# Two raw FFN weight transfers issued ahead of the second batch's v in a fused attention and FFN kernel

## The chip, the cores and the metric

The kernel runs on one core of a Trainium2 chip. Its time is the device time of one execution in microseconds (us), and the kernel before has a median of 1057.45 us in three runs (1054.2 to 1062.04). A profiled execution gives the trace from which all rows below come.

## The reference: what is computed

Three stages follow each other. All arrays are float32, except that the two FFN weights come as float64.

1. Attention on q, k, v of shape (2 batches, 8 heads, 576 positions, 64). Each head adds two attentions: a *pooled* one, on q, k, v averaged over groups of four positions (144 by 144 scores), whose output rows are repeated four times, and a *local* one, in which a position sees only the positions less than four away.
2. An FFN on the 1152 x 512 result: `h = x @ w_in` (512 x 2048), softplus of h, times `w_out` (2048 x 512).
3. Eight experts (512 to 1024 to 512, ReLU), all applied to all tokens and summed with weights P, which come from gate logits by eight rounds of row and column normalization.

## The kernel before

**Stages.** TensorE does the attention of both batches first, then the FFN in four blocks of 512 hidden units, then the experts. The last two take most of the time; the diff touches a load in the attention.

**The attention's units.** Work is cut into units: `pooled(b, hf, p)` (half of the pooled rows, two heads) and `local(b, t, g)` (a tile of 116 positions, four heads). Each has four steps s1 to s4: scores and row maxima and exponentials (`softmax_exp`, VectorE line 306, ScalarE line 309), transposes (TensorE lines 335 and 397, copied by ScalarE at 337 and 399), products with v (lines 344 and 406), and a last transpose (lines 361 and 426). The last step of a pooled unit is copied by ScalarE into `upT` (line 362); that of a local unit is added to it by VectorE into `xf` (line 433, two buffers), which GpSimd splits into two float32r halves of `x` (lines 446 and 447). `emit` lays the units out as a pipeline: with each new unit's s1 come s2 of the unit two back, s3 of the one four back and s4 of the one six back. `fill` and `warm` add products of zeros on TensorE.

**What is hung between the units.** The dictionary `at` holds work to be put in front of the n-th unit: at 1 the q and k of batch 1 (`load_second`), at 9 `load_rest`, at 11 to 14 the pooling of q and k of batch 1 (`pool_qk`), at 16, 19, 23 and 29 the preparation of the first four tiles of FFN weights (`prep`), and from 22 on the first FFN products.

**load_rest.** `load_vd(1)` loads v of batch 1 in two halves `vr` of 80 x 2048 float32 (line 293, 640 KB each) and lets GpSimd add the four positions of each group: line 296 gives `vs`, line 298 the pooled `vd`. The two `vs` lie in the scratch buffers with the tags `ch` and `cs`:

```
s = self.convp.tile([GH, 2, DM], F32, tag=("ch", "cs")[hf], name=f"vs{b}{hf}", bufs=1)
```

`load_raw(1)` issues the loads of the raw weight tiles 0 and 1 (line 117, 1024 KB each, float64 read as pairs of 32-bit words) into two buffers that v of batch 0 has used before them. All four loads are issued by SyncE.

**prep.** `from_double` turns a raw tile into two float32r halves. ScalarE reads it twice, at line 133 into `cs` and at line 135 into `cm`; VectorE works on `cm` (136, 138), then writes `ch` from the raw tile (139), and goes on with 142 to 144; GpSimd ends with line 146 for the first four tiles. `cm`, `ch` and `cs` have one buffer each, which the `vs` of batch 1 share for the latter two. `prep` also orders its work behind a local unit: ScalarE's part behind that unit's copy (line 399), VectorE's behind its add (line 433).

**Who sets the order.** Each engine runs its instructions in a fixed order, which a planner writes when the kernel is built: it goes through the program with durations of its own for every instruction and transfer, and gives each engine, whenever it is free, the first instruction in source order whose inputs and buffers it then reckons to be ready. So an engine's order is not the source's where something comes late by the planner's reckoning. On the chip an instruction that is not ready holds up all that is behind it on its engine.

Of the kernel before, what the change touches and what calls it, by code (L numbers as in the profile page):

```python
# [80 lines left out]
class Net:  # L81
# [660 lines left out]
    def run(self):  # L742
# [52 lines left out]
                self.load_qk(1, p)  # L795

        def load_rest():
            self.load_vd(1)
            self.load_raw(1)

        def prep(n, lag):

# [225 lines left out]
```

## Time and profile before

| | |
|---|---|
| median of three runs | 1057.45 us (1054.2, 1057.45, 1062.04) |
| profiled execution, its own time | 1064.65 us |
| its span, first to last instruction | 1062.9 us |
| TensorE busy | 1050.3 us, 99% of the span |
| VectorE, ScalarE, GpSimd busy | 775.2, 428.7, 162.5 us |
| bytes read by transfers | 60.51 MB |

The page gives the span in 40 slices of 26.6 us, the chain of waits that ended last, and groups of instructions; other views list the instructions of an engine in order of time, or the busy time, the granted TensorE clock and the transfer rate of a stretch. An idle time in brackets is that of the engine just before the instruction, with what ended it. Times count from the span's start.

### The profile page before, as it was taken

Reading aid. Unit: us, or ns where it says so; the run is one execution under the profiler, and the core shown is the slowest. Engines: PE = TensorE matmul, PEld = TensorE weight load, DVE = VectorE, ACT = ScalarE, POOL = GpSimd, SP = SyncE. Lnnn points to the kernel's source line nnn. Section 1 sums busy time; section 2 is a strip of 40 time slices with the busy share of each in tenths; the row PEclk is TensorE's granted clock in tenths of the full one; section 3 lists DMA queues with packets and bytes.
Section 4 is the critical chain, followed back from the end, with each engine's and each line's share of the span. In section 5 each row is a group of like instructions: output and inputs, shape, how many; then the busy total and the mean of one; then the engine's idle time right before and its main releaser. Section 6 shows DMA issues by size and latency. Waiting matters only on the chain.

```text
span 1062.9 us, 16399 instructions
## 1 busy us (share of the span) xinstructions
PE 1050.3 (99%) x6570; PEld 945.1 (89%) x6570; DVE 775.2 (73%) x1470; ACT 428.7 (40%) x815; POOL 162.5 (15%) x210
## 2 busy tenths in 40 slices
PE   8999999999999999999999999999999999999998
PEld 5667999999998899898989989898998989899897
DVE  6578699999987687784947658494765848576572
ACT  5567697776743433241413324141331414133130
POOL 2653300002112220111202011120201112020000
PEclk9789999999999999999999999999999999999999
DMA  9532032222111221111211111121111112110003
GB/s 286 167 97 75 2 119 80 80 80 80 40 40 40 80 80 40 40 41 40 80 40 41 40 40 40 40 81 40 40 40 41 41 40 80 41 40 1 1 2 89
DMA packets 14348, 63.92 MB, mean 60 GB/s; under 512 B 1792, under 2 KB 4608, under 8 KB 7808
## 3 DMA queue, kind: packets, MB, share of 16 engines
q1 hardware_dynamic: 13696, 61.70, 17.9%
q8 instruction: 51, 0.84, 0.3%
q10 hardware_dynamic: 576, 1.18, 0.3%
q14 instruction: 25, 0.20, 0.1%
HBM read 60.51 MB, written 2.36 MB: 59 GB/s over the span
## 4 chain that ended last, share of the span: by engine, by line
PE 89%; DVE 5%; DMA 3%; ACT 2%; issue 1%; SPq 0%; DVEq 0%; ACTq 0%
PE po L613 37%; PE pu L564 33%; PE ph L471 7%; PE py L513 6%; DMA raw<-in_w 1%; DMA k<-in_k 1%; PE pvl L406 1%; PE pl L385 1%; DMA vw<-in_vw 1%; DVE h L492 1%; PE pxl L426 1%; DVE r L488 1%; DVE l L489 1%; DVE yp L525 0%; PE pd L320 0%
## 5 line engine op out<-in xcount | busy, mean ns | idle before, releaser
L564 PE MATMUL pu<-T,a 128*128 128x320 f32 (+1 forms) x2688 | 354.6, 293 | 1.4 <-DVE yp L525 1.4
L564 PEld LDWEIGHTS pu<-T,a 128*128 128x128 f32 x2688 | 351.7, 188 | 3.0 <-issue 1.7
L613 PE MATMUL po<-w,h 128*128 128x512 f32 x960 | 221.3, 390 | 0.0
L635 DVE SCALAR_TENSOR_TENSOR acc<-po,prob,acc 128x512 f32<-128x512 f32 x126 | 94.1, 748 | 173.6 <-PE po L613 173.6
L613 PEld LDWEIGHTS po<-w,h 128*128 128x128 f32 x960 | 179.9, 188 | 37.3
L197 ACT CAST w<-raw 128x1024 fp32r<-128x1024 f32 x32 | 33.4, 1052 | 271.4 <-PE po L613 271.4
L613 PE MATMUL po<-w,h0a 128*128 128x512 f32 x576 | 142.3, 390 | 0.5 <-DVE w L198 0.5
L166 POOL TENSOR_TENSOR s<-raw 128x256 f32<-128x256 f32 x32 | 28.6, 892 | 677.9 <-DVE a L177 472.8
L613 PEld LDWEIGHTS po<-w,h0a 128*128 128x128 f32 x576 | 107.3, 188 | 22.4 <-DVE w L198 0.9
L513 PE MATMUL py<-h,w 128*128 128x384 f32 x576 | 104.0, 336 | 0.6 <-DVE l L490 0.3
L471 PE MATMUL ph<-x,w 128*128 128x384 f32 x576 | 104.4, 336 | 0.0
L513 PEld LDWEIGHTS py<-h,w 128*128 128x128 f32 x576 | 99.7, 188 | 1.7 <-DVE h L492 0.8
L471 PEld LDWEIGHTS ph<-x,w 128*128 128x128 f32 x576 | 99.7, 188 | 0.6 <-issue 0.4
L576 ACT ACTIVATE h<-c 128x320 fp32r<-128x320 f32 x128 | 58.6, 468 | 80.2 <-DVE c L587 80.2
L577 DVE SCALAR_TENSOR_TENSOR h<-c,h 128x320 fp32r<-128x320 f32 x128 | 67.9, 539 | 0.3
L587 DVE TENSOR_TENSOR c<-v,pu 128x256 f32<-128x256 f32 (+1 forms) x128 | 57.6, 450 | 10.9 <-PE pu L564 7.9
L576 ACT ACTIVATE h0a<-c 128x256 fp32r<-128x256 f32 x96 | 37.5, 417 | 50.3 <-DVE c L587 50.0
L198 DVE TENSOR_TENSOR w<-raw,w 128x1024 fp32r<-128x1024 f32 x32 | 39.0, 1219 | 22.1 <-ACT w L197 22.1
L613 PE MATMUL po<-w,h0b 128*128 128x512 f32 x192 | 54.3, 389 | 0.0
L613 PEld LDWEIGHTS po<-w,h0b 128*128 128x128 f32 x192 | 36.0, 188 | 7.5
L585 ACT COPY p<-pu 128x256 f32<-128x256 f32 (+1 forms) x64 | 25.2, 393 | 36.8 <-PE pu L564 35.1
L577 DVE SCALAR_TENSOR_TENSOR h0a<-c,h0a 128x256 fp32r<-128x256 f32 x96 | 39.0, 419 | 0.8 <-ACT h0a L576 0.5
(139 smaller groups left out, 1207.8 us busy)
## 6 DMA issues: line engine op xcount, KB each, us to landing
raw<-in_w SPq DMA_DIRECT2D x48, 1024.0 KB, 4.9
vw<-in_vw SPq DMA_DIRECT2D x20, 130.0 KB, 4.1
vr<-in_vp SPq DMA_DIRECT2D x4, 640.0 KB, 10.3
k<-in_k SPq DMA_DIRECT2D x8, 288.0 KB, 6.6
out<-acc SPq DMA_DIRECT2D x5, 256.0 KB, 2.0
q<-in_q ACTq DMA_DIRECT2D x4, 288.0 KB, 5.9
q<-in_q SPq DMA_DIRECT2D x4, 288.0 KB, 7.1
out<-acc SPq DMA_DIRECT2D x8, 128.0 KB, 2.3
```

Of the source, the lines that this page charges most:

```text
L166: nc.gpsimd.tensor_tensor(s[:, 0], a21, a22, ALU.add)
L197: nc.scalar.copy(w[:, 0], raw)
L198: nc.vector.tensor_tensor(w[:, 1], raw, split(w[:, 0]), ALU.subtract)
L471: nc.tensor.matmul(ps[:, i], lhsT=wv[:, a, k, fo : fo + P], rhs=x[:, b, k], start=(n == 0), stop=(n == 3 * KD - 1),)
L513: nc.tensor.matmul(ps[:, a], lhsT=w[:, i, d * P : (d + 1) * P], rhs=h[:, j, f], start=(n == 0), stop=(n == 3 * NFT - 1),)
L564: nc.tensor.matmul(ps, lhsT=w[:, x, a, k], rhs=t[:, y, b, k], start=(m == 0), stop=(m == 5))
L576: act = nc.scalar.activation(hi, src, AF.Relu)
L577: dve = nc.vector.scalar_tensor_tensor(lo, src, 0.0, split(hi), ALU.max, ALU.subtract)
L585: nc.scalar.copy(to, ps)
L587: nc.vector.tensor_tensor(to, src, ps, ALU.add)
L613: nc.tensor.matmul(ps, lhsT=self.h[s, i, f][:, at * P : (at + 1) * P], rhs=w[:, j], start=(n == 0), stop=(n == 3 * NFT - 1),)
L635: nc.vector.scalar_tensor_tensor(acc, ps, pe, acc, ALU.mult, ALU.add)
```

## The change

Inside `load_rest` the two calls change places, so that the loads of raw weight tiles 0 and 1 stand in front of the loads and additions of the second batch's v. Nothing else is edited.

```
         def load_rest():
+            self.load_raw(1)
             self.load_vd(1)
-            self.load_raw(1)
```

## Rows read from the trace of the kernel before

**Rows 1.** The page's slices: granted TensorE clock in tenths of full speed.
```profile
PEclk9789999999999999999999999999999999999999
```

**Rows 2.** Stretches: from:to, length, busy us of each engine (instructions), granted clock, transfers' share, GB/s.
```profile
38.60:59.02 20.42, 20.42 (x143) 13.27 (x142) 12.80 (x31) 11.13 (x35) 10.86 (x10) 0.50 0.21 66
...
59.02:130.00 70.98, 70.87 (x659) 56.91 (x659) 55.89 (x151) 49.88 (x141) 31.53 (x44) 1.00 0.22 65
...
130.00:160.00 30.00, 30.00 (x175) 30.00 (x174) 29.02 (x36) 26.11 (x32) 0.00 (x0) 1.00 0.32 106
```

**Rows 3.** TensorE in order of time: start, length, line, operation, [idle before, released by].
```profile
24.51 0.27 PE L374 MATMUL pl<-mask,identb 128*128 128x256 bf16 x1
...
33.53 0.28 PE L374 MATMUL pl<-mask,identb 128*128 128x256 bf16 x1
...
35.10 0.66 PE L406 MATMUL pvl<-vw,ptls 128*64 128x130 f32 x8
38.06 0.44 PE L426 MATMUL pxl<-perm,ull 128*128 128x128 f32 x2 [2.29 <-ACT upT L362]
38.60 0.37 PE L374 MATMUL pl<-mask,identb 128*128 128x256 bf16 x1
...
58.66 0.42 PE L374 MATMUL pl<-mask,identb 128*128 128x256 bf16 x1
...
67.33 0.67 PE L344 MATMUL pvd<-vd,ptds 72*72 72x65 f32 x8
...
71.06 0.44 PE L471 MATMUL ph<-x,w 128*128 128x384 f32 x1
```

**Rows 4.** ScalarE in order of time.
```profile
30.81 0.94 ACT L309 ACTIVATE e<-pl,nm 128x64 f32<-128x64 f32 x4
32.99 0.40 ACT L337 COPY ptds<-ptd 72x288 f32<-72x288 f32 x1 [1.24 <-PE ptd L335]
36.77 1.13 ACT L135 ACTIVATE cm<-raw 128x1024 f32<-128x1024 f32 x1 [3.39 <-DMA raw<-in_w]
37.81 0.19 ACT L362 COPY upT<-pxd 128x72 f32<-128x72 f32 x1
...
41.37 1.16 ACT L133 ACTIVATE cs<-raw 128x1024 f32<-128x1024 uint32 x1
```

**Rows 5.** SyncE's queue in order of time: issues merged (x2), from the first's start.
```profile
19.94 2.47 SPq L293 DMA_DIRECT2D vr<-in_vp  x2
22.91 1.09 SPq L117 DMA_DIRECT2D raw<-in_w  x2
```

**Rows 6.** The second raw transfer alone, from issue to landing.
```profile
DMA to landing us min/median/max: 16.1/16.1/16.1
```

**Rows 7.** Stretches again, while v and then the raw tiles pass; last two columns count.
```profile
25.00:31.00 6.00, 5.88 (x73) 4.02 (x71) 2.85 (x10) 4.67 (x18) 0.81 (x2) 1.00 1.00 240
31.00:36.00 5.00, 4.77 (x56) 3.18 (x52) 3.76 (x12) 1.14 (x5) 4.23 (x2) 1.00 1.02 369
```

**Rows 8.** VectorE in order of time.
```profile
16.02 1.22 DVE L296 TENSOR_TENSOR vs<-vr 72x1024 f32<-72x1024 f32 x1 [0.71 <-DMA vr<-in_vp]
...
38.60 0.40 DVE L433 TENSOR_TENSOR xf<-pxl,upT 128x232 f32<-128x232 f32 x1 [2.41 <-ACT e L309]
...
42.56 1.23 DVE L139 SCALAR_TENSOR_TENSOR ch<-raw,cm 128x1024 int32<-128x1024 int32 x1
```

**Rows 9.** GpSimd in order of time.
```profile
31.25 2.35 POOL L296 TENSOR_TENSOR vs<-vr 72x1024 f32<-72x1024 f32 x1 [3.75 <-DMA vr<-in_vp]
34.11 2.34 POOL L296 TENSOR_TENSOR vs<-vr 72x1024 f32<-72x1024 f32 x1 [0.52 <-DMA vr<-in_vp]
36.42 1.27 POOL L298 TENSOR_TENSOR vd<-vs 72x512 f32<-72x512 f32 x1
...
38.40 0.38 POOL L446 CAST x<-xf 128x232 fp32r<-128x232 f32 x1
38.73 1.27 POOL L298 TENSOR_TENSOR vd<-vs 72x512 f32<-72x512 f32 x1
```

## The prediction

> **What bounds the kernel now.** I read the page's slices first, 26.6 us each. TensorE's granted clock is at 9 tenths or more in every slice but the second and third [rows 1], so a change to the opening can act on time in two ways: by a wait, or by the clock. The stretches [rows 2] place the loss: from 38.60 to 59.02 us the granted clock is 0.50 (1.2 of 2.4 GHz), afterwards 1.00, and TensorE is busy for all 20.42 us of it. The list of TensorE in order of time [rows 3] shows what came before the fall: nothing runs between the values of 35.10 and the transposes at 38.06, which record 2.29 us of idle time and name ScalarE as the releaser. ScalarE's list [rows 4] names the source: it is free at 33.39, and its next instruction, line 135 on the first raw weight tile, starts at 36.77 after 3.39 us of idle time ended by the transfer. The copy that TensorE needs stands right behind it and starts at 37.81. SyncE's list [rows 5] has the two transfers of v of batch 1 (line 293) from 19.94 and the two raw ones (line 117) from 22.91 on; each row merges two issues, the second of them some 0.35 us before the row's end. The first raw tile is there at 36.7, the second 16.1 us after its issue at 23.65 [rows 6], at 39.8. They are late because of what is ahead of them: the transfer engines are full from 25 to 36 us, at 240 GB/s while v's 1.31 MB pass and at 369 while the raw 2.1 MB pass [rows 7].
>
> From 130 us on TensorE has no gaps (30.00 of 30.00 us busy, at full clock) [rows 2]. Time won or lost in the opening therefore arrives at the end whole, since all later work is started by work and by no fixed hour.
>
> **The change, part by part.** No instruction is added. Six things move past each other: two raw issues on SyncE go ahead of two v issues, and the four additions of lines 296 and 298 on GpSimd stay where they are in the source, with their data later. The memset of the ones column reads nothing and is not affected.
>
> *Issue slots.* The four SyncE issues take about 0.35 us each [rows 5] in either order, and what is queued behind them on SyncE, the windows of v for the local attention, keeps its slot. A raw tile needs a buffer that v of batch 0 leaves; its second reader on VectorE starts at 16.02 and runs 1.22 us [rows 8], so 17.24 is before the slot at 19.94: no new wait.
>
> *Landing.* v lands at 31.2 and 34.1 (that is when line 296 starts, each after a wait on the transfer) [rows 9], 2.9 us apart; raw follows 2.6 and 3.1 us apart. So the queue reaches v at about 28.3. In the new order I put raw 0 at 28.3 + 2.6 to 3.1 = 30.9 to 31.4, raw 1 at 34, v at 37 and, the bytes being the same, the last at 39.8 as before. Raw 0 is 5.5 us earlier; both v tiles 5.7 us later.
>
> *ScalarE's wait.* With raw 0 there at 31, line 135 (1.13 us) is ready inside the 1.24 us that ScalarE idles between its exponentials (end 31.75) and 32.99 [rows 4]. The 3.39 us wait goes, and so do TensorE's 2.29 us. Bounds: a planner orders the engines by readiness as it foresees it; it placed line 135 where the tile came 3.4 us too late. If it now places it as much too early, the gain is nothing; if it fits, 2.29. I take 2.29, because a free slot lies right behind the new landing.
>
> *The clock.* If TensorE does not stop, I expect it not to fall. What that gives back: five units lie between the starts of the local units at 38.60 and 58.66, 20.06 us or 4.01 each; before the fall, the four from the local unit at 24.51 to that at 33.53 take 9.02, or 2.26 each [rows 3]. Five at 2.26 are 11.3 us, so 20.06 - 11.3 = 8.8 us come back. The lower bound is nothing (the clock falls anyway); a bound between comes from VectorE, which is busy for 12.80 us in the same stretch [rows 2]: if that work must fit, 20.42 - 12.80 = 7.6 us. I take 8.8, since conversion work on VectorE is not wanted by TensorE at once and may slide.
>
> The Trainium skill (TensorE: Matmul & The Clock Gate, Terms) prices throttled time at its length times one minus the granted share; for these 20.42 us at half clock that is an estimate of 10.2 us, and the sum would be 1.4 us better by it. The rows of the units, which contain waits that do not scale with the clock, say 8.8, and I keep them.
>
> *v's own path.* The sums need v at 37 and 39.8: two of 2.35 us and two of 1.27 [rows 9] end at about 43.4 and 44.7 instead of 37.7 and 40.0. The reader on TensorE of the pooled v of batch 1 comes at 67.33 [rows 3], some 56 in the forecast: covered by 11 us. Not covered are two uses of the same scratch. The sums live in the buffers that the weight conversion then writes: line 139 on VectorE (42.56 now [rows 8]) cannot start before the first pooled sum is through, line 133 on ScalarE (41.37 now [rows 4]) not before the second. These are late next. If the planner moves them behind the later v, they cost nothing; if not, see the first rival. Bounds: 0 to 3.8 us of TensorE idle; I take 0.
>
> Sum, against the profiled execution's own time: 1064.65 - 2.3 - 8.8 = 1053.6 us. That execution is 7.2 us above the median of the three runs shown (1057.45), whose lowest is 1054.2; a spread of that size in a kernel that is otherwise saturated is what a half-clock stretch of varying length would give. If the lowest run had no such stretch, only the wait is left to win there: 1054.2 - 2.3 = 1051.9. The two stand near each other, and the forecast between them is **1053 us**, 0.4% under the median.
>
> **Rivals.** *The wait moves to v* (about 1058). At the present spacing VectorE reaches line 139 4.0 us after its add at 38.60 at half clock, some 2.5 at full; without the stop this is 39 to 40. The first sum is through at 43.4, so VectorE would stand for 3 to 4.5 us, with the row maxima of the softmax behind it in order, ScalarE's exponentials behind these and TensorE last. Now 3.39 + 1.13 us of ScalarE's time cost TensorE 2.29, so some 2.2 us are covered; 0.9 to 3.8 us of TensorE idle time would come at 44. With a stop like the present one the clock falls too, and the profiled sum is 1064.65 - 2.29 + (0.9 to 3.8) = 1063.3 to 1066.2, no difference to speak of: 1056 to 1059 on the scale of the median. For it: the transfers are the same bytes in the same full queue, and somebody must be last. Against it: the planner does let readiness decide (it runs line 135 before line 133, against the source), so it can shift lines 133 and 139 too. The Trainium skill (DMA: Bandwidth & Descriptors, Issuing engines are not separate DMA queues) holds that transfers from all queues run on the same engines; by that rule reordering only names another victim, which is this rival.
>
> *GpSimd's queue is blocked* (about 1065, slower). If GpSimd keeps its order, the split of the first attention output (38.40 now) stands behind both additions of line 296 and the first of line 298 [rows 9] and moves 5.7 us to 44.1. The output that it reads has two buffers, so VectorE's third add of this kind (line 433), due at 36.3 + 2 x 2.26 = 40.8, waits until some 46: 5 us, of which 2.2 are covered, so 2.8 of TensorE idle time for the present 2.29. If the clock then stays low up to the first FFN matmuls, the 12 us from 59.02 to 71.06 [rows 3] grow by 12 x (4.01 / 2.26 - 1) = 9.3, and the 5.5 us between 38.6 and 44 at full clock give back 2.4: 1057.45 + 0.5 + 9.3 - 2.4 = 1064.9. It decides if the splits stay behind the v sums; that the first split has its data before v lands in the new order, and so may pass it by readiness, speaks against it.
>
> *The order does not change what ScalarE waits for* (about 1057): the planner places line 135 as much ahead of the new landing as of the old one.
>
> **How the numbers follow.** Forecast 0.45, wait moves to v 0.30, GpSimd blocked 0.14, nothing changes 0.11. The range takes in the forecast with both bounds of the clock term and the two neutral rivals: 1051.9 less 3 for runs on the good side, 1049, up to 1064 for the milder half of the blocked queue. One per cent, about what a measurement of this kernel can tell from no change, is 10.6 us: faster than 1046.9 needs the whole forecast against runs of before as long as the slowest shown, about a third of its 0.45, so 0.16; slower than 1068 is the blocked queue with more idle time than reckoned, most of its 0.14, 0.11; within, 0.73.
>
> **What would show it.** Right: line 135 starts by 33 with no wait for a transfer, TensorE has no gap over 1 us between 30 and 46, the clock is at 1.00 in 40 to 59, the first FFN matmul comes at about 60 instead of 71. Wrong: a gap on TensorE at 40 to 46 behind line 139 or 133 (first rival), the third output add of VectorE waiting on GpSimd (second), line 135 still waiting for its transfer (third), or a clock that falls with no gap ahead of it.

## The result: slower by 0.7%, not faster

The changed kernel takes 1067.9 us (median of 9 executions, 1065.3 to 1069.1); the kernel before 1061.4 (9, 1054.2 to 1063.4). The ratio is 1.0068, interval 1.0044 to 1.0092. The forecast of 1053 us and its range up to 1064 were wrong, and so was the sign.

What the change was to do, it does. SyncE's queue after (start, length, issues merged):

```profile
20.44 1.59 SPq L117 DMA_DIRECT2D raw<-in_w  x2
22.40 1.07 SPq L293 DMA_DIRECT2D vr<-in_vp  x2
```

ScalarE after, against [rows 4]: line 135 runs at 28.70 with no wait ahead of it, and line 133 without one as well.

```profile
28.70 1.14 ACT L135 ACTIVATE cm<-raw 128x1024 f32<-128x1024 f32 x1
...
44.10 1.23 ACT L133 ACTIVATE cs<-raw 128x1024 f32<-128x1024 uint32 x1
```

TensorE after, every instruction of 30 to 110 us with more than 0.5 us of idle time ahead of it (in brackets, with the releaser), against [rows 3]. Line 220 is a product of zeros that `fill` puts in; `uld` (line 356) and `ull` (line 420) are the outputs of a pooled and of a local unit, which VectorE writes and TensorE transposes:

```profile
38.75 0.38 PE L220 MATMUL ptl<-z 128*128 128x512 bf16 x1 [0.51 <-DVE ull L420]
41.98 0.39 PE L220 MATMUL ptl<-z 128*128 128x512 bf16 x1 [0.73 <-DVE uld L356]
48.55 0.59 PE L220 MATMUL pvl<-z 128*128 128x512 bf16 x1 [1.54 <-DVE uld L356]
62.37 2.58 PE L471 MATMUL ph<-x,w 128*128 128x384 f32 x12 [0.69 <-POOL x L446]
77.70 0.44 PE L335 MATMUL ptd<-ident,e 72*72 72x72 f32 x4 [1.55 <-DVE uld L356]
97.71 0.25 PE L361 MATMUL pxd<-ident,uld 72*128 72x72 f32 x1 [1.82 <-DVE uld L356]
```

The one gap of 2.29 us behind ScalarE is gone; six others stand in its place, and five of them wait for VectorE. In the opening TensorE is well ahead: the first FFN matmul comes at 62.37 instead of 71.06. The stretches after (columns as in [rows 2]) show where that went:

```profile
48.75:55.34 6.59, 6.59 (x44) 4.02 (x44) 5.99 (x12) 3.79 (x10) 4.16 (x3) 0.50 0.51 187
55.34:79.22 23.88, 21.64 (x210) 16.08 (x210) 20.38 (x50) 17.15 (x46) 16.16 (x18) 1.00 0.34 111
79.22:85.97 6.75, 6.75 (x39) 5.67 (x40) 3.78 (x13) 3.07 (x9) 0.64 (x1) 0.50 0.17 43
...
99.85:106.73 6.88, 6.88 (x44) 6.08 (x43) 2.30 (x8) 2.44 (x10) 1.28 (x4) 0.51 0.16 41
```

The clock falls to half three times, each time within 2.2 us of the end of one of the three longest gaps, for 6.59 + 6.75 + 6.88 = 20.2 us together, as much as the single 20.42 us of [rows 2]. So in these two executions nothing of the clock is won, and TensorE has more holes. Over the stretch from 30 to 130 us it is idle for 6.84 us instead of 2.50, at a mean granted clock of 0.90 in both; the kernel before, then after:

```profile
30.00:130.00 100.00, 97.50 (x864) 74.24 (x864) 73.06 (x195) 64.51 (x186) 49.22 (x59) 0.90 0.26 83
```

```profile
30.00:130.00 100.00, 93.16 (x840) 72.10 (x841) 77.37 (x189) 60.67 (x178) 49.18 (x57) 0.90 0.25 72
```

Why VectorE is late, its own list and GpSimd's show. VectorE after:

```profile
35.84 2.52 DVE L136 TENSOR_SCALAR cm<-cm 128x1024 f32<-128x1024 f32 x1
38.28 0.41 DVE L420 TENSOR_TENSOR ull<-pvl,rrl 128x256 f32<-128x256 f32 x1
...
38.95 2.18 DVE L138 TENSOR_SCALAR cm<-cm 128x1024 int32<-128x1024 int32 x1
...
45.22 1.74 DVE L142 TENSOR_SCALAR ca<-raw 128x1024 int32<-128x1024 int32 x1
...
74.80 0.41 DVE L306 TENSOR_REDUCE nm<-pl 128x4 f32<-128x256 f32 x1
...
75.42 2.02 DVE L488 SCALAR_TENSOR_TENSOR r<-r,e 128x384 f32<-128x384 f32 x1
77.37 0.28 DVE L356 TENSOR_TENSOR uld<-pvd,rrd 72x128 f32<-72x128 f32 x1
...
94.75 2.61 DVE L488 SCALAR_TENSOR_TENSOR r<-r,e 128x384 f32<-128x384 f32 x1
```

GpSimd after:

```profile
35.46 5.12 POOL L296 TENSOR_TENSOR vs<-vr 72x1024 f32<-72x1024 f32 x2 [2.05 <-DMA vr<-in_vp]
...
74.66 2.37 POOL L146 TENSOR_TENSOR w<-cs,ch 128x1024 fp32r<-128x1024 f32 x1 [5.23 <-DVE ch L144]
...
94.60 2.35 POOL L146 TENSOR_TENSOR w<-cs,ch 128x1024 fp32r<-128x1024 f32 x1 [5.43 <-DVE ch L144]
```

These long instructions of VectorE start while one of GpSimd's is running (35.84 after 35.46; 75.42 after 74.66; 94.75 after 94.60), and the two of line 488 end 0.4 us behind its end (75.42 + 2.02 = 77.44 against 74.66 + 2.37 = 77.03; 97.36 against 96.95). In the kernel before, line 136 takes 0.68 us in three of the first four tiles, and line 488 takes 0.53 to 0.55 us up to 110 us. VectorE before, the first two of line 136:

```profile
38.92 1.63 DVE L136 TENSOR_SCALAR cm<-cm 128x1024 f32<-128x1024 f32 x1
...
55.36 0.68 DVE L136 TENSOR_SCALAR cm<-cm 128x1024 f32<-128x1024 f32 x1
```

Not every instruction of VectorE is held: line 306, which reads PSUM, takes its usual 0.41 us at 74.80, inside the same GpSimd instruction that holds line 488. The attention's small operations stand behind the held ones in VectorE's order. At 78 and 98 us uld comes next and TensorE waits for it; at 48 us VectorE has had no pause since 35.5, has spent 2.52, 2.18 and 1.74 us on lines 136, 138 and 142, which take 0.68 alone, and reaches uld late. That is the theory that the experiments test. The rival: the planner, given earlier raw tiles, puts VectorE's conversion work ahead of the attention's, and this order alone makes TensorE wait.

**Two terms.** The kernels' times spread by up to 10 us from execution to execution, so each execution is split in two below: its *clock loss*, (1 - mean granted clock) x span, and the *rest*, its time less that. This is bookkeeping and not a cause, but it separates the two things that the change touches. The kernel before, 87 executions beside the runs below: clock loss 4.7 us on average (0 to 12.8), rest 1054.4. In 23 of the 87 the clock is at 0.999 or more, with the same program; their mean is 1055.3 us. The split takes off a little too much: over the 87, a straight line through times and losses rises by 0.81 us for each us of clock loss, so a rest measured at much loss comes out too low. The changed kernel: 8.9 and 1058.7. So of its 8.5 us over the mean of the 87 (1067.6 against 1059.1), about half are clock and half stalls (at 0.81 us each, 3.4 and 5.1).

| kernel | ratio to before [interval] | clock loss, us | rest, us |
|---|---|---|---|
| changed kernel | 1.0068 [1.0044, 1.0092] | 8.9 | 1058.7 |
| 1 new transfers, old order | 1.0055 [1.0029, 1.0081] | 9.5 | 1055.5 |
| 2 old transfers, new order | 1.0147 [1.0115, 1.0179] | 13.6 | 1061.6 |
| 3 before, line 135 later | 1.0028 [0.9998, 1.0058] | 7.4 | 1054.8 |
| 4 changed, all cut in four | 1.0038 [1.0019, 1.0057] | 6.8 | 1056.7 |
| 5 changed, line 146 cut | 1.0021 [1.0000, 1.0042] | 3.0 | 1057.6 |
| 6 changed, sums in place | 1.0117 [1.0082, 1.0152] | 12.8 | 1057.7 |
| 7 the same, planned anew | 1.0000 [0.9979, 1.0022] | 3.4 | 1055.2 |
| 8 as 3, sums in place | 0.9971 [0.9951, 0.9992] | 0.6 | 1055.0 |
| 9 as 5, no v sums | 0.9968 [0.9948, 0.9988] | 0.4 | 1055.1 |
| 10 as 8, line 146 cut | 0.9956 [0.9938, 0.9973] | 0.2 | 1055.1 |
| 11 before, line 146 cut | 0.9990 [0.9965, 1.0015] | 3.8 | 1055.2 |

### The profile page after: what moved, and what is told of

Its sections match the earlier page's. It is cut to its first block, busy times and chain, and to the rows that moved or that the text cites. A ratio compares the mean times of both kernels' runs of the same rounds, so it can differ in the third digit from the quotient of the medians.

```text
span 1067.3 us, 16403 instructions
## 1 busy us (share of the span) xinstructions
PE 1049.5 (98%) x6570; PEld 946.2 (89%) x6570; DVE 783.9 (73%) x1470; ACT 429.0 (40%) x815; POOL 164.4 (15%) x210
## 4 chain that ended last, share of the span: by engine, by line
PE 90%; DVE 5%; ACT 2%; DMA 2%; issue 1%; POOL 0%; SPq 0%; ACTq 0%; DVEq 0%
PE po L613 37%; PE pu L564 33%; PE ph L471 8%; PE py L513 7%; PE pvl L406 1%; DMA k<-in_k 1%; PE pl L385 1%; DMA vr<-in_vp 1%; DVE r L488 1%; PE pxl L426 0%; PE pd L320 0%; PE ptl L397 0%; PE pvd L344 0%; DVE cs L143 0%; DVE cm L136 0%
```

## The experiments

All but the seventh hold TensorE, VectorE, ScalarE and GpSimd to an order recorded from one of the two kernels (in runs 3, 8 and 10 with the change of order told there), so that the planner cannot answer the edit: a helper chains each engine's instructions of the opening in that order, without a semaphore.

```diff
             net.run()
+            pin(tc, nc)
```

**Transfers and order apart (1, 2).** The first takes the changed kernel's transfers and the order of before, the second the other pair. The only edit is the order table that the helper chains.

> Raw loads ahead of v in SyncE's queue as in the changed kernel, but TensorE, VectorE, ScalarE and GpSimd run their instructions in exactly the kernel before's order. If the new order of the four engines costs the time (VectorE and GpSimd work placed differently, so that TensorE misses uld three times), the three half-clock stretches go, ScalarE's wait at line 135 is gone, and the time is 0.99 to 1.00 of before. If the transfers themselves cost it (v late, everything behind it late), the time stays 1.005 to 1.010 of before, and waits for the v sums, which now end near 43 us, stand on VectorE and ScalarE at lines 139 and 133.

> v loads ahead of raw as in the kernel before, but the four engines run in exactly the changed kernel's order. If the new order costs the time, the uld gaps and half-clock stretches at 48, 78 and 98 us stand here too and the time is 1.005 to 1.015 of before (ScalarE's line 135 now stands earlier and waits longer for the raw load of 36.7 us, which may add 2 to 10 us). If the order of the transfers costs it, the time is within 0.3% of before.

In the first, ScalarE's wait for raw is gone and so are the gaps for uld and the three half-clock stretches, as the order theory had it; but the wait for v takes their place at once, with one half-clock stretch of 6.8 us (a second one, of 3.4 us at 10.5 us, stands in the traces of both runs ahead of anything that they move; the profiled execution lost 5.3 us of clock, the twelve 9.5 on average). The time, 1.0055, lies in the range of the other theory, so neither expectation came whole. Its TensorE and ScalarE:

```profile
44.82 0.58 PE L220 MATMUL ptl<-z 128*128 128x512 bf16 x1 [4.21 <-ACT e L309]
```

```profile
43.63 0.32 ACT L267 ACTIVATE kd<-kd 128x144 f32<-128x144 f32 x1 [7.69 <-POOL kd L266]
...
46.99 1.15 ACT L133 ACTIVATE cs<-raw 128x1024 f32<-128x1024 uint32 x1 [1.38 <-POOL vd L298]
```

Two things queue behind the late v: GpSimd's line 266 (the pooled k, `kd`) of batch 1, which stands behind the v sums in the old order, and line 133, whose buffer the sums hold. Neither waits in the changed kernel, so its new order does avoid the rival that the prediction put at 0.30. In the second, both prices stand: the gap behind the raw load grows to 4.26 us (2.29 before), and two gaps of the changed kernel follow, those for uld, of 1.55 us at 87 and 1.79 at 107, each with its half clock; the one at 48 us has no counterpart of its size for uld or ull (1.03 at most).

```profile
38.82 0.38 PE L361 MATMUL pxd<-ident,uld 72*128 72x72 f32 x1 [4.26 <-ACT upT L362]
...
87.33 0.45 PE L335 MATMUL ptd<-ident,e 72*72 72x72 f32 x4 [1.55 <-DVE uld L356]
107.34 0.26 PE L361 MATMUL pxd<-ident,uld 72*128 72x72 f32 x1 [1.79 <-DVE uld L356]
```

So the later gaps travel with the order and not with the transfers. Why that order makes gaps is the next question.

**The forecast's gain, without touching transfers (3).** ScalarE's order in the kernel before, with the late tile's line 135 one unit later (in shorthand, a name for each instruction); VectorE's first line 136 stands behind the next lines 420 and 306 to match:

```diff
-ptds, cm (L135), upT, e(pd), ptls, kd, e(pl), kd, ptds, cs (L133)
+ptds, upT, e(pd), ptls, e(pl), cm (L135), kd, kd, ptds, cs (L133)
```

> The kernel before with its own transfers and order; only ScalarE's first line 135 stands one local unit later, behind the raw load's landing at 36.7 us, and VectorE's first line 136 a few small operations later. The prediction's theory (the wait and the half clock behind it are the whole price): ScalarE's 3.39 us wait is under 0.5 us, TensorE's 2.29 us gap at 36 us is gone, the clock stays at 1.00 up to 130 us, and the time falls by 2.3 to 11 us, 0.990 to 0.998 of before. The theory that VectorE, held up while GpSimd runs a long instruction, is what binds in this stretch: the gap at 36 us goes, but another gap of 1 to 2 us that ends on VectorE follows before 110 us, the clock falls there, and the time is 0.998 to 1.004 of before.

Line 135 no longer waits, but everything is now some 2.9 us earlier (VectorE's add at 35.71 instead of 38.60), and line 133 runs into the v sums, although v is not late here. ScalarE, then TensorE:

```profile
41.08 1.14 ACT L133 ACTIVATE cs<-raw 128x1024 f32<-128x1024 uint32 x1 [2.41 <-POOL vd L298]
```

```profile
43.09 0.69 PE L426 MATMUL pxl<-perm,ull 128*128 128x128 f32 x2 [3.32 <-ACT e L309]
```

The time lies in the second theory's range, but the mechanism is a miss for both: the wait behind the one removed is neither raw's nor VectorE's, but that of the buffer which [rows 4] could not show, because line 133 came there just after the sums.

**GpSimd's instructions cut in four (4, 5).** The changed kernel in its own order; the same work in shorter pieces, in run 4 both the v sums and line 146, in run 5 line 146 alone. Lines of these two kernels are shifted (136 is 143, 138 is 145, 488 is 514 in run 4 and 501 in run 5). The cut of line 146, in short form:

```diff
-        e.tensor_tensor(w[:, 1], s, h, ALU.mult)
+        c = 256 if n < NFT else 1024
+        for o in range(0, 1024, c):
+            e.tensor_tensor(w[:, 1, o : o + c], s[:, o : o + c], h[:, o : o + c], ALU.mult)
```

> The changed kernel, transfers and engine order, with GpSimd's long instructions of the first 110 us (the second batch's v sums, and the multiply of line 146 for the first four raw tiles) each cut into four pieces of the same total work. If VectorE's instructions are held until the instruction that GpSimd is running ends, VectorE's longest at lines 136 and 488 fall from 2.5 us to 1.3 us or less, TensorE's gaps for uld at 48, 78 and 98 us fall under 0.7 us, at least two of the three half-clock stretches vanish, and the time is 0.992 to 1.000 of before. If the hold follows GpSimd's total work, or the order of VectorE's own work makes the gaps, the gaps stay at 1.5 us or more and the time at 1.004 to 1.010 of before.

> The changed kernel and its engine order; only GpSimd's multiply of line 146 (first four raw tiles) is cut into four pieces, the second batch's v sums stay whole. Taking clock loss of a run as (1 - granted clock) x span and the rest as its time less that: the changed kernel had 8.9 us of loss and a rest of 1058.7 us, the kernel before 4.4 and 1054.7. If VectorE is held while one GpSimd instruction runs, the two gaps for uld at 78 and 98 us fall from 1.55 and 1.82 us to 0.6 us or less and their half-clock stretches mostly go, the first one at 48 us stays at 1.5 us: rest 1056 to 1057.5, time 1.002 to 1.006 of before. If the order of VectorE's own work makes these gaps, they stay and the time is 1.0068 as in the changed kernel.

VectorE in run 4:

```profile
36.08 1.07 DVE L143 TENSOR_SCALAR cm<-cm 128x1024 f32<-128x1024 f32 x1
...
37.74 1.23 DVE L145 TENSOR_SCALAR cm<-cm 128x1024 int32<-128x1024 int32 x1
...
76.61 1.08 DVE L514 SCALAR_TENSOR_TENSOR r<-r,e 128x384 f32<-128x384 f32 x1
```

The hold follows the single GpSimd instruction, not GpSimd's total work: 2.52 to 1.07, 2.18 to 1.23, 2.02 to 1.08 us, with VectorE's order unchanged. The gaps for uld at 42 and 98 us go, that at 48 falls from 1.54 to 0.62 and that at 78 from 1.55 to 0.61. What run 4 loses again is the sums' length: in pieces, they take 6.42 + 4.77 us instead of 5.12 + 2.48, lines 139 and 133 wait 2.84 and 4.57 us for their buffers, and TensorE has a new gap behind them, longer than any of the changed kernel's:

```profile
48.81 0.41 PE L233 MATMUL ptl<-z 128*128 128x512 bf16 x1 [3.48 <-ACT ptls L425]
```

So its time, 1.0038, lies in neither range. Run 5 leaves the sums whole, and the split is clean. TensorE in run 5:

```profile
49.13 0.38 PE L233 MATMUL pvl<-z 128*128 128x512 bf16 x1 [1.54 <-DVE uld L369]
...
75.64 0.45 PE L348 MATMUL ptd<-ident,e 72*72 72x72 f32 x4 [0.60 <-DVE uld L369]
```

The gap behind the sums stays at 1.54, the two behind line 146 fall to 0.60 and to nothing, and clock loss falls from 8.9 to 3.0 us. The mean time falls by 7.0 us (1067.6 to 1060.6), or by 0.5% as the two ratios to the kernel before have it.

**The v sums in place (6, 7).** The second batch's sums are written over the loaded v, so that no conversion waits for their buffer; run 6 in the changed kernel's order, run 7 as the planner orders it anew.

```diff
-            s = self.convp.tile([GH, 2, DM], F32, tag=("ch", "cs")[hf], name=f"vs{b}{hf}", bufs=1)
+            if b == 0:
+                s = self.convp.tile([GH, 2, DM], F32, tag=("ch", "cs")[hf], name=f"vs{b}{hf}", bufs=1)
+            else:
+                s = r[:GH, 0:2]
```

> The changed kernel and its engine order; the second batch's v sums are written over the loaded v instead of into the two buffers that the conversion of the raw tiles also uses, so the conversion's lines 139 and 133 no longer wait for the v sums. If the late v sums (to 43.8 us) make the gap at 48 us by holding the conversion, which stands ahead of the attention on VectorE and ScalarE, VectorE's line 139 starts at 40 us instead of 43.1, the 1.54 us gap at 48 us is under 0.7 us, and the rest falls by 1 to 2 us; the gaps at 78 and 98 us stay: time 1.003 to 1.006 of before. If the buffer has nothing to do with it, gap and time stay as in the changed kernel, 1.0068.

> The changed kernel with the v sums in place, and the engines in the order that its planner now gives (it places the conversion freely, since nothing waits for the v sums). If the shared buffers and the order that follows from them are the price of the late v, the time falls below the changed kernel's: 0.995 to 1.003 of before. If GpSimd's long instructions beside VectorE decide, gaps of 1.5 us for uld stand wherever a line 136 or 488 meets a GpSimd instruction, and the time is 1.004 to 1.010.

Run 6 is slower than both expectations, and the way is instructive. The gap at 48 us went, but an earlier and longer one came, because now line 136 stood through both additions of line 296, which ran without a pause between them. VectorE, GpSimd and TensorE:

```profile
36.00 4.62 DVE L136 TENSOR_SCALAR cm<-cm 128x1024 f32<-128x1024 f32 x1
```

```profile
35.43 4.64 POOL L299 TENSOR_TENSOR vr<-vr 72x1024 f32<-72x1024 f32 x2 [1.86 <-DMA vr<-in_vp]
```

```profile
41.01 0.59 PE L220 MATMUL ptl<-z 128*128 128x512 bf16 x1 [2.62 <-DVE ull L423]
```

In the changed kernel VectorE came in between the two (line 136 ends at 38.36, with the sums taking 5.12 us in all); why it does not here is open. Run 7 gets rid of the two holds of line 488 by another plan alone, keeps one gap of 2.57 us for uld at 44 us behind the sums, and comes out level with the kernel before. That the changed kernel's plan has line 488 held twice is thus an accident of this plan.

The starts in the profile do not always tell which of the two engines will be held. In the kernel before, as in run 7, line 146 starts first, yet line 488 keeps its 0.54 us and GpSimd's instruction is the longer one. GpSimd and VectorE before:

```profile
97.13 2.98 POOL L146 TENSOR_TENSOR w<-cs,ch 128x1024 fp32r<-128x1024 f32 x1
```

```profile
97.34 0.54 DVE L488 SCALAR_TENSOR_TENSOR r<-r,e 128x384 f32<-128x384 f32 x1
```

**Neither hold (9).** Run 5 with this edit (136 is 143, 138 is 145). It leaves out the second batch's v sums and sets the pooled v to ones, so it computes something else and serves only to tell the causes apart:

```diff
-        nc.gpsimd.memset(vd[:, :, :, D:DA], 1.0)
+        nc.gpsimd.memset(vd if b else vd[:, :, :, D:DA], 1.0)
...
+            if b == 1:
+                continue
```

> The changed kernel and its engine order with line 146's multiply cut into four pieces (as in the earlier run of that alone, which measured a rest of 1057.6 us and 3.0 us of clock loss, and kept the 1.54 us gap for uld at 49 us behind a line 136 of 2.73 us and a line 138 of 2.18 us), and without the second batch's v sums: its v is set to ones and the four additions on GpSimd are left out; v is still transferred. If GpSimd's v sums hold VectorE up and so make the gaps of 0.72, 0.72 and 1.54 us at 39, 42 and 49 us, VectorE's first line 136 and 138 take 0.7 to 1.2 us, the three gaps are under 0.5 us each, no half clock before 110 us, and rest and time are 1053 to 1055 us. If the planner's order of VectorE's own work makes them, lines 136 and 138 get short, but the gaps stay and the rest stays at 1057 us or more.

VectorE's first two conversion steps, and the stretch from 30 to 130 us:

```profile
36.19 0.68 DVE L143 TENSOR_SCALAR cm<-cm 128x1024 f32<-128x1024 f32 x1
...
37.45 0.68 DVE L145 TENSOR_SCALAR cm<-cm 128x1024 int32<-128x1024 int32 x1
```

```profile
30.00:130.00 100.00, 98.34 (x914) 78.76 (x912) 80.98 (x205) 69.24 (x192) 43.68 (x67) 0.98 0.29 84
```

The order is the changed kernel's, the gaps at 39, 42 and 49 us are gone, and TensorE is busy for 98.34 us instead of 93.16. So the order of VectorE's work does not make the gaps. The edit also frees the sums' two buffers and their place in GpSimd's queue; but in run 5 neither line 139 nor line 133 waits for those buffers at the first tile, and VectorE, which TensorE waits for, shows no idle time from 35.5 to 52.7 us. And v is still transferred, so the transfer does not lengthen VectorE's instructions. What is left is the hold. A small half-clock stretch after a gap of 0.61 us at 71.5 was not expected.

**The version that beats both (8, 10), and a control (11).** Run 8 is run 3 with the sums in place, run 10 that with line 146 cut, run 11 the kernel before with the cut alone.

> The kernel before with ScalarE's first line 135 one local unit later (as in the earlier run of that, where ScalarE then waited 2.41 us for the v sums at line 133 and TensorE 3.32 us behind it), now with the v sums in place, so that line 133 waits for nothing. If the two waits of ScalarE, for raw and then for the v sums' buffer, are the whole price of this stretch, neither gap stands, the clock stays at 1.00 from 30 to 130 us, clock loss is 0 to 2 us in most runs (4.4 before), the rest is 1051 to 1053 us and the time 0.992 to 0.997 of before: a version faster than both. If VectorE, held beside GpSimd, binds next, a gap of 1 to 2 us for uld follows at 42 to 55 us and the time is 0.998 to 1.004.

> The fastest so far (kernel before, ScalarE's first line 135 one unit later, v sums in place: 0.9971 of before, clock 1.00) with line 146 of the first four raw tiles cut into four pieces. If the hold beside GpSimd makes what gaps are left, VectorE's line 136 of 2.15 us at 46.6 us falls to 1.3 us or less, the 1.09 us gap at 53 us is under 0.6 us, and the time is 0.995 to 0.997 of before. If that gap comes from VectorE's order, it stays and the time is as without the cut, 0.997.

> A control: the kernel before and its own engine order, with nothing but line 146's multiply cut into four pieces. If the cut only helps where a long VectorE instruction that TensorE waits behind meets it, nothing changes here, where no TensorE gap over 0.3 us follows such a meeting: 0.998 to 1.002 of before. If the cut frees time wherever it stands, or costs some by its overhead, the time is 0.994 to 0.998 or 1.002 to 1.005.

In run 8 the clock stays up as expected, but three gaps of 0.43 to 1.09 us stay, and the rest, 1055.0, is not down to the 1051 to 1053 expected. The stretch of run 10, and what gaps over 0.3 us are left on its TensorE before 110 us:

```profile
30.00:130.00 100.00, 97.15 (x916) 77.97 (x915) 81.29 (x206) 71.11 (x193) 53.84 (x71) 1.00 0.29 92
```

```profile
40.67 0.44 PE L442 MATMUL pxl<-perm,ull 128*128 128x128 f32 x2 [0.86 <-ACT e L325]
45.62 0.44 PE L442 MATMUL pxl<-perm,ull 128*128 128x128 f32 x2 [0.38 <-DVE ull L436]
51.00 0.44 PE L442 MATMUL pxl<-perm,ull 128*128 128x128 f32 x2 [0.68 <-DVE ch L146]
75.45 0.39 PE L233 MATMUL pvl<-z 128*128 128x512 bf16 x1 [0.82 <-DVE uld L372]
```

The clock stays up, and run 10 has the lowest median with nothing left out: 1055.2 us, all 12 executions between 1054.8 and 1056.2. Line 136 falls from 2.15 to 1.20 us as expected; the gap that was 1.09 us falls to 0.68, which now ends on a wait for a conversion buffer, and one of 0.82 is new. Its gain over the kernel before is the clock loss and nothing else: its mean, 1055.3, is that of the 23 executions of before at full clock. Whether the cut adds to run 8 is not shown, since the two intervals overlap. The control is level, as it should be where no TensorE gap hangs on the hold.

## Why the prediction was wrong

*Issue slots, landing, ScalarE's wait: right in the main.* No new wait stands at the issues. Everything lands some 2 us earlier than reckoned: line 135 had its tile by 28.70 instead of the 30.9 to 31.4 forecast, and v's first sum starts at 35.46 instead of 37. The wait of 3.39 us and TensorE's gap at 36 us are gone.

*The clock: this step failed.* It took 8.8 us on two grounds, that TensorE would not stop, and that VectorE's conversion work "is not wanted by TensorE at once and may slide". The second ground does not hold, and with it falls the first: VectorE runs in order, line 136 stands ahead of ull and uld, and in its new place beside the v sums it takes 2.52 us instead of the 1.63 it took before. TensorE stops six times, for 6.84 us between 30 and 130 us instead of 2.50, and the clock falls three times. Two of the signs that it named for being right do come, line 135 by 33 us and no gap over 1 us between 30 and 46; the first long gap stands just behind that stretch, at 48. Where TensorE does not stop for long the clock does stay up, as the prediction had it (runs 8 and 10). The middle bound from VectorE's busy time (12.80 of 20.42 us) counted its durations as fixed; with v later and raw earlier the two meet, and runs 4, 5 and 9 show that the meeting is the price. The profile had a hint: one instruction, line 136, with 1.63 us beside a GpSimd addition and 0.68 elsewhere.

The Trainium skill (SBUF — State Buffer, Who interferes with whom) states this as a rule for some instructions of VectorE, those in a two-port mode, which `tensor_scalar` can enter, and those with two inputs in SBUF: they share a port pair with GpSimd as an exclusive lock, whoever issues first has it for the whole instruction, and the other is blocked, not slowed. Most rows agree: line 136, a `tensor_scalar`, goes from 0.68 to 2.52 or 4.62 us, line 488, with two inputs, from 0.54 to 2.61, each ending 0.4 to 0.6 us behind GpSimd's instruction where the end of that one is shown, line 306 keeps its 0.41, and with GpSimd's work in pieces line 136 takes 1.07. It works the other way round too: in run 3 the second line 298 takes 2.27 us instead of 1.27. Who issues first no run shows: by the starts in the profile, line 146 at 97.13 of the kernel before should have held line 488 and did not.

*The size of the clock term.* For the profiled execution 8.8 us is about right: its 20.42 us at half clock, 10.2 us of clock loss, come to 8.3 at the 0.81 of the 87 executions. (The two groups of units behind the 8.8 are not alike, four local and one pooled unit against two and two; in like units the trace gives about 8.2.) But even with the clock up, 8.8 us were not there to be won from the median. The profiled execution of before had 10.6 us of clock loss, the mean of 87 has 4.7, and run 10, which has none, wins 4.2 us against the executions of before that stood beside it (means 1055.3 and 1059.5).

*The 2.3 us of the wait: not kept.* At full clock runs 8 to 10 take 1055.2 to 1055.3 us on average, and so do the 23 executions of before (1055.3). In run 10 four gaps of 0.38 to 0.86 us (2.74 together) replace the one of 2.29. That time won in the opening arrives at the end is not refuted by this: from 130 to 1040 us TensorE is idle for 3.6 us in run 10 and for 3.4 in the kernel before. In the order of the changed kernel it is 4.7 us, of which 1.3 stand at 149.5 and have no counterpart in the kernel before, so there some of its loss comes after 130 us.

*v's own path: right as far as it went.* The planner moved lines 139 and 133 behind the sums at no wait, as the 0 taken for them supposed. What the sums run beside on VectorE was not priced.

*The rivals.* "The wait moves to v" is real in the old order (run 1: 4.21 us, a little over its 0.9 to 3.8), but the new plan avoids it. "GpSimd's queue is blocked" did not come: the first split runs at 32.28, ahead of the sums. The slower side came by a mechanism that was not on the list.

## What to carry to other kernels

When a transfer order moves, look not only at who waits for the late data but at what the late work will then run beside: here GpSimd's sums and VectorE's conversion changed from following each other to meeting. If an instruction on VectorE has one duration far above its siblings, see what GpSimd was running, and price each long GpSimd instruction at up to its whole length for those of VectorE's that showed the hold and may start just after it. Take the size of a clock term from several executions and not from the profiled one.

## What the runs showed of the hardware

The length of a half-clock stretch did not follow the gap ahead of it. In the profiled executions a gap of 2.29 us is followed by 20.4 us at half clock (before), one of 3.32 us by 13.6 (run 3), three of 1.54 to 1.82 us by 6.6 to 6.9 each (changed kernel), one of 1.51 by 20.5 (run 11), one of 2.62 by 3.4 (run 6); in run 1 the clock fell inside the gap of 4.21 us and was back 6.8 us later; one of 0.61 us by 3.4 us (run 9), and three of 0.43 to 1.09 us (run 8) and four of 0.38 to 0.86 (run 10) by none. The same program of before ran 23 of 87 times with a mean clock of 0.999 or more. What decides is open.

The cut of line 146 costs GpSimd 2.8 to 4.0 us for what took 2.35 to 2.98 in one piece, and still pays where VectorE stands behind it (run 5).
